# A memory-recurrent attention layer with a gMLP: a split first weight transfer with a warmed TensorE, second waits moved to earlier matmuls, and the context evacuated in eight pieces

## The chip, the cores and the metric

The kernel runs on one core of one Trainium2 chip. The metric is the device time of one execution in microseconds (us). Most executions of one kernel agree within 0.3 per cent, which here is 2.6 us, so single microseconds need several executions.

## The reference, cut to what matters

```python
h  = x + A(layernorm(x))            # x: 1 x 2048 x 512, bf16
h2 = h + B(layernorm(h))

# A: 64 segments of 32 rows, one after the other
for s in range(64):
    hs = concat([mem, xs[s]])                    # 8 memory rows + 32 rows
    q, k, v = hs @ Wq, hs @ Wk, hs @ Wv          # 32 heads of 128
    p = softmax(mask(q @ k.T * 128**-0.5))
    o = (p @ v) @ Wo                             # 40 x 512
    mem = o[:8]                                  # the next segment needs it
    outs.append(o[8:])

# B: gelu(x @ w_in), layernorm of one half, a 2048 x 2048 product along the rows,
#    a gate, and w_out
```

A is a chain: segment s+1 cannot start before the eight memory rows of segment s are there. Everything that does not depend on the memory (the products of the x rows with Wq, Wk and Wv) is done ahead, in the opening for the first 32 segments and as fill between the dependent products later.

## The kernel before: the parts that the change and the argument touch

The kernel writes its own dependencies. Each operation is recorded with the tokens it reads and writes; the waits are worked out at the end. An instruction carries one wait itself; for each further one a separate semaphore instruction is emitted ahead of it.

```python
def emit(self, eng_name, eng, sems, dma_sems):
    for op in self.by_eng[eng_name]:
        for d in op.waits:
            ...                                  # eng.wait_ge(semaphore, value), one per wait
        ins = op.fn(eng)
```

The opening: two x tiles, then the weights in pieces of 1 MB, all issued on the SP queue; two layernorms, whose inverse root runs on POOL; transposes, and one copy per tile.

```python
load_xe(0, 0)
load_xe(1, 1)
for hq in range(4):
    load_w(0, hq)                                # Wq, 1 MB each
...
for j in range(2):
    ln_stats(j)
for j in range(2):
    ln_apply(j)
    xT(j, 6 + j)                                 # four 128 x 128 transposes
    xe_copy(j, 6 + j)                            # one ACT copy
for i in range(8):                               # Q products of both chunks of 16 segments
    for ck in range(2):
        start_group(qkx_mm, qkx_evac, ck, i)
for n in range(8):                               # V products of the first chunk
    ...
    start_v(0, n)
```

The V products (`vx_mm`) are evacuated by ACT and DVE in turn into one of eight rows of a buffer, `part`, and stored to memory from there (`vext_d`).

The end of a step: the probabilities times V (`PV_half`, with 16 matmuls on V and 4 on Vx, the V rows of x, for each half b of the heads), the evacuation of the context into `cT`, the output projection (`Wo`).

```python
PV_half(s, 0)
PV_half(s, 1)
for f in xs[2:4]: f()                            # fill: products of x rows of a later chunk
fill(nw2)
cT_evac(0, "act", (0,))
cT_evac(2, "dve", (0,))
cT_evac(0, "act", (1,))
cT_evac(2, "dve", (1,))
cT_evac(1, "act")                                # both halves, 320 columns
cT_evac(3, "dve")
...
Wo(WOQ, OB, 0, OC)                               # columns 0 to 255, eight quads in the order WOQ
part_evac(s, OB, 0, OC)
Wo(WOQ[:6], OB2, OC, D)
```

## Time and profile before

| | before |
|---|---|
| time, median of 4 executions beside the changed kernel | 868.14 us (867.4 to 869.19) |
| span of the profiled execution | 866.1 us |
| first product of the opening | 7.82 us |
| first V product | 24.51 us |
| first matmul of step 0 | 55.12 us |
| last Vx quad of step 0 to that of step 63 | 623.5 us, the usual step 9.82 us |
| last Vx quad to the last matmul (the MLP) | 176.0 us |
| last matmul to the end | 4.1 us |

The lines that carry these readings stand in the prediction below. How to read it: TensorE's own order of instructions makes 96 per cent of the chain of work that ends last, so what counts is when each quad of matmuls (four column tiles, run together) starts, and not how long an engine is busy. I number the steps from 0 and count a step from the start of its last Vx quad to that of the next step's.

### The profile page before, as it was taken

Reading aid. Unit: us, or ns where it says so; the run is one execution under the profiler, and the core shown is the slowest. Engines: PE = TensorE matmul, PEld = TensorE weight load, DVE = VectorE, ACT = ScalarE, POOL = GpSimd, SP = SyncE. Lnnn points to the kernel's source line nnn. Section 1 sums busy time; section 2 is a strip of 40 time slices with the busy share of each in tenths; the row PEclk is TensorE's granted clock in tenths of the full one; section 3 lists DMA queues with packets and bytes.
Section 4 is the critical chain, followed back from the end, with each engine's and each line's share of the span. In section 5 each row is a group of like instructions: output and inputs, shape, how many; then the busy total and the mean of one; then the engine's idle time right before and its main releaser. Section 6 shows DMA issues by size and latency. Waiting matters only on the chain.

```text
span 866.1 us, 45456 instructions
## 1 busy us (share of the span) xinstructions
PE 849.6 (98%) x22453; PEld 433.9 (50%) x18876; DVE 501.8 (58%) x1246; ACT 467.4 (54%) x1291; POOL 158.6 (18%) x427
## 2 busy tenths in 40 slices
PE   6999999999999999999999999999999999999998
PEld 6664445454445544455445554454554444444443
DVE  3446666666666666666666666566655564363343
ACT  3445666666666666666666666666666655400000
POOL 1621212121212212121211221121211122100000
PEclk9999999999999999999999999999999999999999
DMA  9972232213141211222241313342211690032101
GB/s 323 380 218 72 69 74 74 64 42 85 26 92 29 78 38 50 77 70 57 68 85 31 92 41 93 62 92 58 59 51 42 193 274 16 1 104 77 64 13 39
DMA packets 114180, 75.20 MB, mean 87 GB/s; under 512 B 70712, under 2 KB 99520, under 8 KB 113984
## 3 DMA queue, kind: packets, MB, share of 16 engines
q1 hardware_dynamic: 113840, 72.19, 30.4%
q8 instruction: 164, 2.69, 1.3%
q14 instruction: 32, 0.26, 0.1%
q10 hardware_dynamic: 144, 0.07, 0.0%
HBM read 39.46 MB, written 20.58 MB: 69 GB/s over the span
## 4 chain that ended last, share of the span: by engine, by line
PE 96%; DVE 2%; DMA 1%; issue 1%; SPq 0%; ACT 0%
PE f_ps L280 30%; PE f_ps L660 14%; PE f_ps L281 13%; PE f_ps L1092 11%; PE f_ps L426 3%; PE f_ps L710 3%; PE f_ps L461 3%; PE f_ps L1166 3%; PE f_ps L1054 3%; PE f_ps L574 3%; PE f_ps L1085 3%; PE f_ps L625 3%; PE f_ps L631 1%; PE f_ps L554 1%; PE f_ps L681 1%; DMA f_arena<-in_A_Wq_dram 1%
## 5 line engine op out<-in xcount | busy, mean ns | idle before, releaser
L280 PE MATMUL f_ps<-f_arena,f_hT 128*32 128x512 bf16 (+1 forms) x5120 | 352.8, 337 | 1.7 <-issue 0.5
L281 PE MATMUL f_ps<-f_arena,f_hT 128*32 128x256 bf16 (+1 forms) x3072 | 214.5, 308 | 0.0
L280 PEld LDWEIGHTS f_ps<-f_arena,f_hT 128*32 128x32 bf16 x5120 | 121.0, 96 | 168.8 <-issue 85.6
L518 ACT ACTIVATE f_Tst<-f_ps 128x512 bf16<-128x512 f32 (+1 forms) x320 | 149.9, 510 | 57.6 <-PE f_ps L280 53.9
L660 PE MATMUL f_ps<-f_arena,f_cT 128*32 128x256 bf16 x4096 | 134.6, 273 | 1.4 <-ACT f_cT L645 1.1
L597 POOL TENSOR_TENSOR f_E_sb<-f_R_sb,f_E_sb 128x64 bf16<-128x64 f32 x128 | 48.2, 377 | 378.5 <-ACT f_R_sb L589 378.5
L526 DVE STREAM_TRANSPOSE f_QT<-f_Tst 128x256 uint32<-128x256 uint32 x128 | 57.1, 446 | 94.9 <-ACT f_Tst L518 94.9
L660 PEld LDWEIGHTS f_ps<-f_arena,f_cT 128*32 128x32 bf16 x4096 | 92.7, 95 | 35.6 <-ACT f_cT L645 21.2
L1092 PE MATMUL f_ps<-f_arena 128*128 128x512 bf16 x448 | 100.6, 379 | 0.0
L617 DVE TENSOR_SCALAR f_V_sb<-f_ps 128x512 bf16<-128x512 f32 (+1 forms) x128 | 70.6, 551 | 41.1 <-PE f_ps L280 41.1
L672 ACT ACTIVATE f_part<-f_ps 128x256 bf16<-128x256 f32 x128 | 49.2, 384 | 68.2 <-PE f_ps L660 68.2
L647 DVE TENSOR_SCALAR f_cT<-f_ps 128x160 bf16<-128x160 f32 (+1 forms) x192 | 61.0, 373 | 38.0 <-PE f_ps L631 38.0
L645 ACT ACTIVATE f_cT<-f_ps 128x160 bf16<-128x160 f32 (+1 forms) x192 | 53.0, 348 | 38.9 <-PE f_ps L631 38.9
L1092 PEld LDWEIGHTS f_ps<-f_arena 128*128 128x128 bf16 x448 | 43.8, 98 | 52.7
L526 DVE STREAM_TRANSPOSE f_KT<-f_Tst 128x128 uint32<-128x128 uint32 (+1 forms) x192 | 66.0, 356 | 2.7
L585 ACT ACTIVATE f_R_sb<-f_ps 128x160 f32<-128x160 f32 x128 | 38.9, 304 | 33.5 <-PE f_ps L281 25.6
L1098 DVE TENSOR_TENSOR f_arena<-f_ps,f_arena 128x512 f32<-128x512 f32 x28 | 19.3, 689 | 54.4 <-PE f_ps L1092 52.4
L567 ACT ACTIVATE f_E_sb<-f_ps 128x224 bf16<-128x224 f32 x128 | 45.7, 357 | 0.1
L593 DVE TENSOR_TENSOR f_E_sb<-f_R_sb,f_E_sb 128x160 bf16<-128x160 f32 x128 | 44.7, 350 | 0.0
L589 ACT ACTIVATE f_R_sb<-f_R_sb 128x160 f32<-128x160 f32 x128 | 42.6, 333 | 2.0
L710 PE MATMUL f_ps<-f_arena,f_cTx 128*32 128x512 bf16 x512 | 40.6, 380 | 0.0
L280 PE MATMUL f_ps<-f_arena,f_hTe 128*32 128x512 bf16 x512 | 39.0, 382 | 0.0
(105 smaller groups left out, 1026.7 us busy)
## 6 DMA issues: line engine op xcount, KB each, us to landing
wT_d<-f_wst SPq DMA_DIRECT2D x32, 256.0 KB, 2.7
f_arena<-wT_d SPq DMA_DIRECT2D x32, 256.0 KB, 4.6
f_arena<-in_A_Wq_dram SPq DMA_DIRECT2D x4, 1024.0 KB
f_arena<-in_A_Wv_dram SPq DMA_DIRECT2D x4, 1024.0 KB
f_arena<-in_A_Wk_dram SPq DMA_DIRECT2D x4, 1024.0 KB, 16.0
f_arena<-in_A_Wo_dram SPq DMA_DIRECT2D x4, 1024.0 KB
f_Vx<-vext_d SPq DMA_DIRECT2D x128, 32.0 KB
f_xn<-in_A_x_dram SPq DMA_DIRECT2D x16, 128.0 KB, 2.7
```

Source lines behind the costliest of these rows:

```text
L280: return e.matmul(out, lhsT=lhsT, rhs=rhs, start=start, stop=stop, skip_group_check=True, tile_position=pos)
L281: return e.add_instruction(mybir.InstMatmult(name=nc.get_next_instruction_name(), engine=mybir.EngineType.PE, ins=[e.lower_ap(rhs), e.lowe ...
L518: act(lambda e: e.activation(out=st_.rearrange("p (hp i r) -> p hp i r", i=32, r=2), in_=ps[:, bank, 0:64 * np_].rearrange("p (hp r i) -> ...
L526: dve(lambda e: e.transpose(out=dst, in_=src), reads=tok, writes=[(nm, b, k) for k in halves(b, p0, np_)])
L597: pool(lambda e: e.tensor_tensor(out=ev, in0=rv, in1=ev, op=ALU.mult), reads=[("R", b), ("Ex", b)], writes=[("Ex", b)])
L617: dve(lambda e: e.tensor_scalar(out=dst, in0=src, scalar1=VSC, scalar2=None, op0=ALU.mult), reads=[PB(bank)], writes=tok)
L645: act(lambda e: e.activation(out=dst, in_=src, func=ACT.Copy, scale=UNSC), reads=[PB(PVB[c])], writes=tok)
L647: dve(lambda e: e.tensor_scalar(out=dst, in0=src, scalar1=UNSC, scalar2=None, op0=ALU.mult), reads=[PB(PVB[c])], writes=tok)
L660: pe(lambda e, h=h, g=g, i=i, b=b, c=c: e.matmul(ps[32 * g:32 * g + 32, bank, 0:d1 - d0], lhsT=cTh[:, i, 8:40], rhs=w_o[:, h, d0:d1], star ...
L672: act(lambda e: e.activation(out=part[:, s % 8, d0:d1], in_=ps[:, bank, 0:d1 - d0], func=ACT.Copy), reads=[PB(bank)], writes=[("part", s % ...
L710: pe(lambda e, h=h, g=g, i=8 * qr + bg: e.matmul(ps[32 * g:32 * g + 32, WXB, :], lhsT=cTx[:, rb % 2, i, :], rhs=w_o[:, h, :], start=(i < 4 ...
L1092: pe(lambda e: e.matmul(ps[:, bank, 0:TB], lhsT=z2[:, sc, fb * 128:(fb + 1) * 128], rhs=wTb[tb % 2][:, :, sc, :], start=(sc == 0), stop=(s ...
```

## The change

Its intent is to shorten three things: the opening's start, the wait of the output projection for the context, and the semaphore instructions on TensorE. The core of the diff:

```diff
+        pe = self.by_eng["pe"]
+        for op in pe:
+            while len(op.waits) > 1:
+                d = op.waits[-1]
+                t = next((p for p in reversed(pe[max(0, op.pos - 60):op.pos]) if not p.waits and p.gidx > d.gidx), None)
+                if t is None:
+                    break
+                op.waits.pop()
+                t.waits = [d]
...
+        if mi == 0 and hq == 0:                 # the first Wq piece in two halves of 0.5 MB
+            cm = c0 + 4 * DH
+            sp(lambda e, c0=c0: e.dma_start(ws[:, :, c0:cm], wr[:, :, c0:cm]), writes=["W0"])
...
+    load_xe(1, 1, "act")
     load_xe(0, 0)
-    load_xe(1, 1)
...
+    for _ in range(44):                         # warming matmuls on ones
+        pe(lambda e: e.matmul(ps[:, 1, 0:128], lhsT=onesrc[:, 0:128], rhs=onesrc[:, 0:128], ...
+    ln_bn(0)
+    ln_root(0)                                  # inverse root on ACT: Ln, then Exp of -0.5 of it
...
+    xe_halves(0, 0, (6, 7))                     # half copies on ACT and DVE
...
+        if ck == 1 and n < 4:                   # half of the second chunk's V brought forward,
+            t, tok = (hbuf, xo)[n // 2]...      # into other buffers
...
-    WOQ = ((0, 0), (2, 0), (0, 1), (2, 1), (1, 0), (1, 1), (3, 0), (3, 1))
+    WOQ = ((0, 0), (2, 0), (0, 1), (2, 1), (1, 0), (3, 0), (1, 1), (3, 1))
...
-        cT_evac(1, "act")
-        cT_evac(3, "dve")
+        cT_evac(1, "act", (0,))
+        cT_evac(3, "dve", (0,))
+        cT_evac(1, "act", (1,))
+        cT_evac(3, "dve", (1,))
```

Below, the first block is called the carried waits, the last two (`WOQ` and the evacuations) the pieces, and all between them the opening.

More of the change, by code (lines that the diff above doesn't have):

```diff
@@ L305, in xbuf, with load_xe @@
         return (xn[:, j, :], [("xn", j)]) if j < 2 else (part[:, j, :], [("part", j, 0), ("part", j, 1)])
-    def load_xe(ck, j):
+    def load_xe(ck, j, q="sp"):
         t, tok = xbuf(j)
-        sp(lambda e: e.dma_start(t, xe[CK * ck:CK * ck + CK, XM:SEG, :]), writes=tok)
+        em.add(q, lambda e: e.dma_start(t, xe[CK * ck:CK * ck + CK, XM:SEG, :]), writes=tok, dma=True)
     def load_w(mi, hq):
@@ L314, in load_w @@
         c0, c1 = hq * 8 * DH, (hq + 1) * 8 * DH
+        if mi == 0 and hq == 0:
+            cm = c0 + 4 * DH
+            sp(lambda e, c0=c0: e.dma_start(ws[:, :, c0:cm], wr[:, :, c0:cm]), writes=["W0"])
+            em.mark_const("W0")
+            c0 = cm
         sp(lambda e: e.dma_start(ws[:, :, c0:c1], wr[:, :, c0:c1]), writes=[("W", mi, hq)])
         em.mark_const(("W", mi, hq))
+    load_xe(1, 1, "act")
     load_xe(0, 0)
-    load_xe(1, 1)
     for hq in range(4):
@@ L358, in late_consts, with ln_bn @@
         pool(lambda e: e.tensor_copy(out=mask[:, 224:448], in_=mask[:, 0:224]), reads=["mask"], writes=["mask"])
-    def ln_stats(j):
+    def ln_bn(j):
         t, tok = xbuf(j)
@@ L364, in ln_stats, with ln_root @@
         dve(lambda e: e.bn_stats(out=st1[:, k, :], in_=t), reads=tok, writes=[("st1", k)])
+    def ln_root(j):
+        k = j % 3
+        dve(lambda e: e.bn_aggr(out=mv1[:, k, :], in_=st1[:, k, :]), reads=[("st1", k)], writes=[("mv1", k)])
+        act(lambda e: e.activation(out=rs1[:, k:k + 1], in_=mv1[:, k, 1:2], func=ACT.Ln, bias=EPS), reads=[("mv1", k)], writes=[("rs1", k)])
+        act(lambda e: e.activation(out=rs1[:, k:k + 1], in_=rs1[:, k:k + 1], func=ACT.Exp, scale=-0.5), reads=[("rs1", k)], writes=[("rs1", k)])
+    def ln_stats(j):
+        k = j % 3
+        ln_bn(j)
         dve(lambda e: e.bn_aggr(out=mv1[:, k, :], in_=st1[:, k, :]), reads=[("st1", k)], writes=[("mv1", k)])
@@ L379, in ln_inplace, with xT @@
         ln_apply(j)
-    def xT(j, bank):
+    def xT(j, bank, dcs=range(DC)):
         t, tok = xbuf(j)
-        for dc in range(DC):
+        for dc in dcs:
             pe(lambda e, dc=dc: e.transpose(out=psb[:, bank, dc * 128:(dc + 1) * 128], in_=t[:, dc * 128:(dc + 1) * 128],
@@ L393, in x_flip @@
         sp(lambda e: e.dma_start(xs_d[i], t), reads=rd, writes=[("xs", i)])
-        sp(lambda e: e.dma_start_transpose(out=dst, in_=xs_d[i]), reads=[("xs", i)], writes=[tok])
+        sp(lambda e: e.dma_start_transpose(out=dst, in_=xs_d[i]), reads=[("xs", i)], writes=tok)
     def ring_fill(rb):
@@ L408, in xe_copy, with xe_halves @@
         src = psb[:, bank, 0:512].rearrange("p (dc c) -> p dc c", dc=DC)
-        act(lambda e: e.activation(out=hTe[:, ck % 3, :, :], in_=src, func=ACT.Copy), reads=[PB(bank)], writes=[("hTe", ck % 3)])
+        act(lambda e: e.activation(out=hTe[:, ck % 3, :, :], in_=src, func=ACT.Copy), reads=[PB(bank)],
+            writes=[("hTe", ck % 3, 0), ("hTe", ck % 3, 1)])
+    def xe_halves(ck, j, banks):
+        for hf in range(2):
+            xT(j, banks[hf], (2 * hf, 2 * hf + 1))
+        for hf in range(2):
+            src = psb[:, banks[hf], 256 * hf:256 * hf + 256].rearrange("p (dc c) -> p dc c", dc=2)
+            dst = hTe[:, ck, 2 * hf:2 * hf + 2, :]
+            if hf == 0:
+                act(lambda e, dst=dst, src=src: e.activation(out=dst, in_=src, func=ACT.Copy), reads=[PB(banks[0])], writes=[("hTe", ck, 0)])
+            else:
+                dve(lambda e, dst=dst, src=src: e.tensor_copy(out=dst, in_=src), reads=[PB(banks[1])], writes=[("hTe", ck, 1)])
     def mem0_transpose(bank):
@@ L417, in mem0_transpose, with qkx_mm @@
         act(lambda e: e.activation(out=hT[:, 0, :, 0:M], in_=src, func=ACT.Copy), reads=[PB(bank)], writes=[("hTm", 0, 0), ("hTm", 0, 1)])
-    def qkx_mm(ck, i, bank):
+    def qkx_mm(ck, i, bank, hhs=range(4)):
         mi, q = i // 8, i % 8
         ws = (w_q, w_k)[mi]
-        for hh in range(4):
+        for hh in hhs:
+            wt = "W0" if i < 2 and hh < 2 else ("W", mi, q // 2)
             h = 8 * (q // 2) + 2 * hh + q % 2
@@ L427, in qkx_mm @@
                                                          rhs=hTe[:, ck % 3, dc, :], start=(dc == 0), stop=(dc == DC - 1)),
-                   reads=[("hTe", ck % 3), ("W", mi, q // 2)], writes=[PB(bank)])
+                   reads=[("hTe", ck % 3, dc // 2), wt], writes=[PB(bank)])
     def qkx_evac(ck, i, bank, eng="act"):
@@ L445, in qkx_rows @@
                                           dc == 0, dc == DC - 1, (0, 32 * c)),
-               reads=[("hTe", ck % 3), ("W", mi, 2 * b), ("W", mi, 2 * b + 1)], writes=[PB(bank)])
+               reads=[("hTe", ck % 3, dc // 2), ("W", mi, 2 * b), ("W", mi, 2 * b + 1)], writes=[PB(bank)])
     def qkx_flip(ck, mi, r, b, bank):
@@ L462, in vx_mm @@
                                                        start=(dc == 0), stop=(dc == DC - 1), tile_position=(0, 32 * c)),
-                   reads=[("hTe", ck % 3), ("W", 2, n // 2)], writes=[PB(bank)])
+                   reads=[("hTe", ck % 3, dc // 2), ("W", 2, n // 2)], writes=[PB(bank)])
     def vx_evac(ck, n, bank, eng="act"):
-        if ck < 2:
+        if ck == 1 and n < 4:
+            t, tok = (hbuf, xo)[n // 2][:, n % 2, :], [(("h", "xo")[n // 2], n % 2)]
+        elif ck < 2:
             t, tok = part[:, n, :], [("part", n, 0), ("part", n, 1)]
@@ L758, in fast_path @@
     act(lambda e: e.preload_act_table_set("natural_log_exp_and_others"))
-    for j in range(2):
-        ln_stats(j)
-    for j in range(2):
-        ln_apply(j)
-        xT(j, 6 + j)
-        xe_copy(j, 6 + j)
+    for _ in range(44):
+        pe(lambda e: e.matmul(ps[:, 1, 0:128], lhsT=onesrc[:, 0:128], rhs=onesrc[:, 0:128], start=True, stop=True), reads=["onesrc"], writes=[PB(1)])
+    ln_bn(0)
+    ln_root(0)
+    ln_bn(1)
+    ln_apply(0)
+    ln_root(1)
+    xe_halves(0, 0, (6, 7))
+    ln_apply(1)
+    for hp in range(2):
+        for i in range(2):
+            qkx_mm(0, i, 2 + i, (2 * hp, 2 * hp + 1))
+        if hp == 0:
+            xe_halves(1, 1, (0, 1))
+    qkx_evac(0, 0, 2, "act")
+    qkx_evac(0, 1, 3, "dve")
+    for i in range(2):
+        qkx_mm(1, i, 4 + i)
+        qkx_evac(1, i, 4 + i, ("act", "dve")[i])
     for mi in (2, 1):
@@ L785, in start_v @@
         start_group(vx_mm, vx_evac, ck, n)
-    for i in range(8):
+    for i in range(2, 8):
         for ck in range(2):
@@ L797, in fast_path @@
         start_v(0, n)
-        if n == 1:
+        if n % 2 == 1:
+            start_v(1, n // 2)
+        if n == 2:
             xT(4, 6)
             ring_copy(0, 6)
-        if n == 2:
+        if n == 3:
             xT(5, 7)
             ring_copy(1, 7)
-        if n == 3:
+        if n == 4:
             xT(6, 6)
@@ L814, in fast_path @@
             start_group(qkx_mm, qkx_evac, ck, i)
-    for n in range(8):
+    for n in range(4, 8):
         start_v(1, n)
-        if n % 4 == 3:
-            load_wo(2 + n // 4)
+        if n % 2 == 1:
+            load_wo(n // 2)
     for i in range(12, 16):
@@ L985, in fast_path @@
         if j4 == 1 and 2 <= rb + 2 < RB:
-            late.append(lambda rb=rb: (ln_apply(0), x_flip(0, rb, xn[:, 1, :].rearrange("p (dc c) -> p dc c", dc=DC), ("xn", 1))))
+            late.append(lambda rb=rb: (ln_apply(0), x_flip(0, rb, xn[:, 1, :].rearrange("p (dc c) -> p dc c", dc=DC), [("xn", 1)])))
         if s == 2:
@@ L989, in fast_path @@
         if s == 3:
-            late.append(lambda: (ln_apply(7), x_flip(7, RB, hTe[:, 0, :, :], ("hTe", 0))))
+            late.append(lambda: (ln_apply(7), x_flip(7, RB, hTe[:, 0, :, :], [("hTe", 0, 0), ("hTe", 0, 1)])))
         if j4 == 1 and rb >= 2:
```

## The prediction

> **What bounds the kernel now.** I read the page's first three parts, then the windows by stage, then the timeline of the opening and of one recurrent step, then the rows of single lines.
>
> ```profile
> PE 849.6 (98%) x22453; PEld 433.9 (50%) x18876; DVE 501.8 (58%) x1246; ACT 467.4 (54%) x1291; POOL 158.6 (18%) x427
> DMA  9972232213141211222241313342211690032101
> PE 96%; DVE 2%; DMA 1%; issue 1%; SPq 0%; ACT 0%
> ...
> 0.00:55.10 55.10, 48.02 (x792) 38.78 (x792) 21.95 (x38) 20.66 (x31) 20.05 (x78) 1.00 0.97 329
> 55.10:691.00 635.90, 631.37 (x20834) 316.20 (x17252) 398.44 (x1062) 412.76 (x1201) 122.79 (x315) 1.00 0.28 69
> 691.00:866.10 175.10, 170.25 (x833) 78.95 (x832) 81.41 (x147) 33.97 (x60) 15.78 (x34) 1.00 0.27 77
> ```
>
> TensorE's instruction order sets the end (96% of the chain). The opening projections take 55 us with DMA full (0.97); then 64 recurrent steps take 636 us; the MLP takes 175 us. "PE busy" hides bubbles, since matmul ends are modelled, so I went by the starts of matmuls: four column tiles run together, and such a quad of 512 columns is followed by the next after 215 ns, one of 256 after 109, one of 40 after 25, one of 64 after 28. Anything more is a bubble. A usual step takes 9.81 us. Its middle:
>
> ```profile
> 319.95 0.45 POOL L597 TENSOR_TENSOR f_E_sb<-f_R_sb,f_E_sb 128x64 bf16<-128x64 f32 x1 [0.51 <-ACT f_R_sb L589]
> 320.30 0.21 PE L631 MATMUL f_ps<-f_E_sb,f_Vx 32*128 32x64 bf16 x4
> 320.33 0.28 PE L625 MATMUL f_ps<-f_E_sb,f_V_sb 32*128 32x40 bf16 x16
> 320.50 0.21 PE L631 MATMUL f_ps<-f_E_sb,f_Vx 32*128 32x64 bf16 x4
> 320.73 0.83 ACT L645 ACTIVATE f_cT<-f_ps 128x160 bf16<-128x160 f32 x3 [0.58 <-PE f_ps L631]
> 320.80 0.95 DVE L647 TENSOR_SCALAR f_cT<-f_ps 128x160 bf16<-128x160 f32 x3 [0.57 <-PE f_ps L631]
> 321.08 1.14 PE L660 MATMUL f_ps<-f_arena,f_cT 128*32 128x256 bf16 x32
> ...
> L158 PEldq EVENT_SEMAPHORE  x167: 51/51/51, 7.7 to 822.3; - x167
> L160 PEldq EVENT_SEMAPHORE  x52: 51/51/51, 28.6 to 694.7; - x52
> L645 ACT ACTIVATE f_cT<-f_ps x192: 297/304/444, 62.8 to 686.6; 128x160 bf16<-128x160 f32 x128, 128x320 bf16<-128x320 f32 x64
> L647 DVE TENSOR_SCALAR f_cT<-f_ps x192: 311/325/482, 62.8 to 686.8; 128x160 bf16<-128x160 f32 x128, 128x320 bf16<-128x320 f32 x64
> ```
>
> See two things. The PV products (L625, L631) end in quads that wait for two semaphores, and TensorE has 219 separate semaphore instructions of 51 ns. And the output projection (L660) starts while ACT and DVE are still evacuating the context: its fifth quad starts 186 ns after the fourth (median of 64 steps), not 109, because it waits for ACT's 320-wide piece.
>
> The opening:
>
> ```profile
> 3.49 0.69 DVE L364 BATCH_NORM_STATS2 f_st<-f_xn 128x6 f32<-128x512 bf16 x1 [3.49 <-DMA f_xn<-in_A_x_dram]
> 4.80 0.57 POOL L368 TENSOR_TENSOR f_rs<-f_rs,f_mhalf 128x1 f32<-128x1 f32 x1
> 7.05 0.61 PE L384 MATMUL f_ps<-f_ident,f_xn 128*128 128x128 bf16 x4 [0.57 <-DVE f_xn L374]
> 7.82 6.38 PE L426 MATMUL f_ps<-f_hTe,f_arena 128*128 128x128 bf16 x70 [0.16 <-DMA f_arena<-in_A_Wq_dram]
> ...
> 26.90 0.40 PE L384 MATMUL f_ps<-f_ident,f_part 128*128 128x128 bf16 x4 [0.48 <-DVE f_part L374]
> ```
>
> The first projection waits for 1 MB of Wq until 7.82. Its matmuls start 107 ns apart until 12.7 us, then 56. At 26.04 the last V quad starts, and TensorE waits for DVE's normalization until 26.90.
>
> **What the skill says.** "TensorE: Matmul & The Clock Gate", Part 1: the array runs at half clock until about 3.4 us of sustained activity, in a free-running window, 107 ns a 128-column matmul cold and 56 warm. The trace agrees: 107, then 56, the change 4.9 us after the dense run began. "Perfetto Trace Analysis", Identifying Dependency Chains: instructions that wait on several engines may get EventSemaphore instructions put before them. Agrees: 219 on TensorE, 51 ns each. "VectorE: DVE Perf Modes", the errata section, gives a PSUM read a fixed part plus one cycle an element (172 + FD for ScalarE, 120 + FD for VectorE). Agrees in kind: ACT 304 ns for 160 columns and 443 for 320, so splitting a piece should repeat some 165 ns; but consecutive 160-wide pieces start 184 to 200 ns apart on ACT and 236 on DVE, so most of the fixed part overlaps the neighbour.
>
> **The change, part by part.**
>
> *Eight pieces.* ACT did 160, 160, 320; now 160 four times; DVE likewise; the projection takes the halves in the order in which they come. In the step at 410 us: the first quad starts at .068; ACT starts its third piece at .091, DVE at .246. Split, ACT's halves end near .39 and .57, DVE's near .56 and .80; 0.055 later TensorE may go. Quads four to eight are due at .51, .62, .73 and .84: the first three are ready, the last comes at .85. So the ninth quad, the first of the second half of the columns, starts some 65 to 75 ns earlier than now, where the fifth starts at .587 instead of .51. ACT and DVE finish 40 and 70 ns later; ACT's next work after a projection flip leaves 234 ns before the part evacuation, which moves 75 nearer: enough. 64 x 0.070 = 4.5 us.
>
> *Carried waits.* A second wait is moved to an earlier matmul that had none, so the 51 ns instruction goes. In a step three matmuls have two waits. The one before the scores is hidden under 256-column quads (109 to the next: no bubble). The two at L631 show as 79 ns instead of 25: 54 each, 108 a step. But the work behind them has its own clock. In usual steps the second half's PV starts 101 ns after DVE's normalization ends, where 57 is what a bound start shows; and the last L631 starts 108 ns after POOL's multiply (L597), where bound steps show 60 and without the instruction some 57. So of 97 to 108 ns only about 51 can come out before POOL bounds. About 34 usual steps give 51; some 4 with POOL early give 97; every fourth step (already bound by DVE and POOL) gives about 8; about 10 whose Vx load is late give nothing. 1.7 + 0.4 + 0.1 = 2.2 us; I take 2.0. The context's evacuation follows L631 directly (0.58 to the projection, with or without fill between), so this passes on.
>
> *Opening.* The x tiles are issued on two queues, Wq's first half MB comes alone and is issued 0.6 us earlier, and the inverse root goes from POOL (0.22 + 0.57 and hops) to two ACT operations of about 0.2 (estimate from ACT's smallest rows, 0.18 to 0.19). x at 3.49, statistics to 4.40, root to 4.95, apply 0.41 to 5.4. The 44 warm matmuls run from about 1.08 for 44 x 0.107 = 4.7, to 5.8, so the transposes go at 5.8 and, after half-width copies on ACT and DVE, the first product at about 6.6 (Wq's half MB near 5.8, an estimate from 7.7 for a whole one). That is 1.2 earlier than 7.82. Cold matmuls cost before (12.7 - 7.8)/2 = 2.4; after, the gate should open between 4.5 and 7.9 by the skill's window, so about 0.2 remains: 2.2. V groups of the second chunk fill the wait at 26.04: 0.65. One transpose group now stands in the stream: -0.25. Sum 3.8 us. All matmul work is the same; the rest of the file is not touched.
>
> Together 3.8 + 4.5 + 2.0 = 10.3 us: **868.4 - 10.3 = 858.1**, say 858.
>
> **Rivals.** (1) The opening is held by the loads. For: DMA is at 0.97 and about 386 GB/s until 44 us; the third Wk piece landed at 37.2, pieces are 2.7 us apart, so Wv's first is in near 20 and TensorE will want it at 21. Also the first Wq wait is now carried to the fourth transpose, so a late Wq holds the second copy too. Against: bringing forward half of the second V delays the want for Wk by 3.5 us. If it wins, the opening gives 1.5 to 2 and the time is 860. (2) POOL doesn't bind, and the carried waits give all 108 ns: 6.9 us, time 853.5. Against: bound steps show its 60 ns clearly. Or a wait met costs the same wherever it stands, and they give nothing: 860. (3) The extra two evacuations push ACT and DVE so that the last half comes late: every 10 ns is 0.6 us, and if nothing is won, 862.5. Against: the starts above. (4) The whole is hidden because the recurrence is bound by another engine: 866 or no change; against, DVE and ACT are at 63 to 65% in the steps and wait for TensorE.
>
> **Range and chances.** Independent doubts: opening +-1.5, pieces +-1, waits +-2, Vx loads +-1: together about 3. 855 to 861.5 holds it 8 times in 10. Two per cent is 17.4 us, to 851: it needs rival 2 and more; 0.03. Slower by 2%: 0.01. Same: 0.96.
>
> **What would show it.** First projection at 6.6 and all 56 ns apart from about 6 to 7 us; the opening ending at 51.3 instead of 55.1; no wait for Wv or Wk. In a step: the fifth L660 quad 109 to 120 ns after the fourth, and the ninth some 75 ns earlier than now, counted from the first; semaphore instructions on TensorE nearly gone; the last Vx product 57 ns after POOL's multiply; a usual step at 9.69 instead of 9.81. I am wrong if the last Vx quad starts less than 57 ns after POOL, if a new bubble stands at the eighth quad, or if the MLP's 175 us move.

## The result, and the profile after

The changed kernel took 860.87 us (median of four, 858.82 to 863.35), against 868.14. The ratio is 0.9917, with a 95 per cent interval of 0.9888 to 0.9945; ratios here are the mean time of a kernel's executions over that of the executions of before in the same rounds, so not quite the ratio of the medians. The predicted 858.0 is 2.9 us too low, and the time lies in the range of 855 to 861.5. Of the 10.3 us promised, about 7.3 came.

The page of the changed kernel, first part, the DMA row and the chain:

```profile
PE 845.2 (98%) x22497; PEld 427.6 (50%) x18920; DVE 506.4 (59%) x1312; ACT 471.7 (55%) x1359; POOL 156.3 (18%) x423
DMA  8983222213041211322241313243231690032101
PE 96%; DMA 2%; DVE 1%; issue 0%; SPq 0%; ACT 0%; DVEq 0%
```

See that TensorE still carries 96 per cent, but that DMA has come up from 1 to 2 per cent of the chain. The windows by stage (columns: stretch, its length, busy time and instruction count of PE, PEld, DVE, ACT and POOL, granted clock, DMA share, GB/s):

```profile
0.00:54.44 54.44, 50.43 (x836) 40.78 (x836) 22.32 (x40) 20.89 (x35) 18.26 (x74) 1.00 0.95 323
54.44:683.34 628.90, 624.67 (x20838) 307.89 (x17256) 402.75 (x1126) 416.94 (x1265) 122.34 (x315) 1.00 0.28 70
683.34:859.10 175.76, 170.15 (x833) 78.88 (x832) 81.34 (x147) 33.87 (x60) 15.75 (x34) 1.00 0.26 77
```

The opening, promised at 51.3, ends at 54.4: it gave 0.7 us of the 3.8. The steps gave 7.0, where 6.5 had been promised. The last stretch is 0.7 us longer, but not in the MLP: its matmuls take 175.9 us as before, and the end after the last matmul takes 4.8 us instead of 4.1. That end is between 4.1 and 5.2 us in all traces, without pattern. One usual step in the changed kernel, its middle, to be laid beside the step in the prediction:

```profile
317.17 0.44 POOL L636 TENSOR_TENSOR f_E_sb<-f_R_sb,f_E_sb 128x64 bf16<-128x64 f32 x1 [0.52 <-ACT f_R_sb L628]
...
317.40 0.27 PE L664 MATMUL f_ps<-f_E_sb,f_V_sb 32*128 32x40 bf16 x16
...
317.51 0.20 PE L670 MATMUL f_ps<-f_E_sb,f_Vx 32*128 32x64 bf16 x4
...
317.54 0.29 PE L664 MATMUL f_ps<-f_E_sb,f_V_sb 32*128 32x40 bf16 x16
...
317.67 0.21 PE L670 MATMUL f_ps<-f_E_sb,f_Vx 32*128 32x64 bf16 x4
...
317.95 0.89 ACT L684 ACTIVATE f_cT<-f_ps 128x160 bf16<-128x160 f32 x4 [0.58 <-PE f_ps L670]
318.02 1.02 DVE L686 TENSOR_SCALAR f_cT<-f_ps 128x160 bf16<-128x160 f32 x4 [0.57 <-PE f_ps L670]
...
318.30 1.19 PE L699 MATMUL f_ps<-f_arena,f_cT 128*32 128x256 bf16 x36
```

In the step before, the two Vx quads (L631 there, L670 here) start 0.20 us apart, here 0.16: 40 ns are gone. POOL's multiply ends at 317.61 and the last Vx quad starts at 317.67, 56 ns later, so it is bound by POOL, as foretold. But now look at what follows. ACT takes the context up at 320.73 − 320.50 = 0.23 us after that quad's start before, and at 317.95 − 317.67 = 0.28 us after it here. The 40 ns did not reach the evacuation. The rows of the evacuation by form:

```profile
L684 ACT ACTIVATE f_cT<-f_ps x256: 297/308/323, 62.1 to 679.1; 128x160 bf16<-128x160 f32 x128
L686 DVE TENSOR_SCALAR f_cT<-f_ps x256: 311/315/326, 62.2 to 679.3; 128x160 bf16<-128x160 f32 x128
```

All 256 pieces on each engine are now 160 columns wide and none lasts over 326 ns. There are no semaphore instructions left on TensorE: the rows of that instruction list other engines only.

The chain of waits of the opening of the changed kernel (start, length, what):

```profile
2.41 6.83 DMA f_arena<-in_A_Wq_dram
9.24 0.05 issue
9.29 13.65 PE f_ps L463 x240
...
40.46 6.79 DMA vext_d<-f_part
47.26 0.03 issue
...
47.36 0.70 DVE f_part L512
48.06 0.05 issue
48.10 6.43 PE f_ps L463 x112
```

Two transfers stand in it: the second half of the first Wq piece, where the chain before had the whole piece (from 2.16, 5.52 us long), and a store to memory, which the chain before did not have. The first product starts at 6.83, a microsecond earlier than before, but TensorE then waits until 9.24 for the second half of the split piece. And at 46.5 it stops for 1.6 us (the 1.36 in the view below counts from a modelled end), because DVE and ACT may not write over rows of `part` whose store has not landed:

```profile
44.21 0.60 ACT L510 ACTIVATE f_part<-f_ps 128x512 bf16<-128x512 f32 x1 [2.15 <-DMA vext_d<-f_part]
...
47.36 0.69 DVE L512 TENSOR_SCALAR f_part<-f_ps 128x512 bf16<-128x512 f32 x1 [4.40 <-DMA vext_d<-f_part]
...
48.10 1.07 PE L463 MATMUL f_ps<-f_hTe,f_arena 128*128 128x128 bf16 x16 [1.36 <-DVE f_part L512]
```

That store was issued at 40.46, right behind 1 MB of Wo, and landed at 47.26.

### The profile page after: what moved, and what is told of

Its sections match the earlier page's. It is cut to its first block, busy times and chain, and to the rows that moved or that the text cites. A ratio compares the mean times of both kernels' runs of the same rounds, so it can differ in the third digit from the quotient of the medians.

```text
span 859.1 us, 45449 instructions
## 1 busy us (share of the span) xinstructions
PE 845.2 (98%) x22497; PEld 427.6 (50%) x18920; DVE 506.4 (59%) x1312; ACT 471.7 (55%) x1359; POOL 156.3 (18%) x423
## 4 chain that ended last, share of the span: by engine, by line
PE 96%; DMA 2%; DVE 1%; issue 0%; SPq 0%; ACT 0%; DVEq 0%
PE f_ps L289 30%; PE f_ps L699 13%; PE f_ps L290 13%; PE f_ps L1148 11%; PE f_ps L749 3%; PE f_ps L498 3%; PE f_ps L463 3%; PE f_ps L664 3%; PE f_ps L1222 3%; PE f_ps L1110 3%; PE f_ps L613 3%; PE f_ps L1141 3%; PE f_ps L593 1%; PE f_ps L670 1%; DMA f_arena<-in_A_Wq_dram 1%; DMA vext_d<-f_part 1%
## 5 line engine op out<-in xcount | busy, mean ns | idle before, releaser
L699 PE MATMUL f_ps<-f_arena,f_cT 128*32 128x256 bf16 x4096 | 130.0, 274 | 1.3 <-ACT f_cT L684 1.1
L699 PEld LDWEIGHTS f_ps<-f_arena,f_cT 128*32 128x32 bf16 x4096 | 90.2, 94 | 35.3 <-ACT f_cT L684 22.9
L686 DVE TENSOR_SCALAR f_cT<-f_ps 128x160 bf16<-128x160 f32 x256 | 65.1, 317 | 36.4 <-PE f_ps L670 36.4
L684 ACT ACTIVATE f_cT<-f_ps 128x160 bf16<-128x160 f32 x256 | 57.1, 309 | 36.9 <-PE f_ps L670 36.9
L1154 DVE TENSOR_TENSOR f_arena<-f_ps,f_arena 128x512 f32<-128x512 f32 x28 | 19.3, 690 | 54.4 <-PE f_ps L1148 52.4
```

The costliest lines, as they stand in the source:

```text
L684: act(lambda e: e.activation(out=dst, in_=src, func=ACT.Copy, scale=UNSC), reads=[PB(PVB[c])], writes=tok)
L686: dve(lambda e: e.tensor_scalar(out=dst, in0=src, scalar1=UNSC, scalar2=None, op0=ALU.mult), reads=[PB(PVB[c])], writes=tok)
L699: pe(lambda e, h=h, g=g, i=i, b=b, c=c: e.matmul(ps[32 * g:32 * g + 32, bank, 0:d1 - d0], lhsT=cTh[:, i, 8:40], rhs=w_o[:, h, d0:d1], star ...
```

## The experiments

Twelve runs followed, on four chips, and all gave correct results. Kernels are compared only within the same rounds. This table has them in one place; "gain" is (1 − ratio) times 868 us, and the last two columns are from the profiled execution of each, in us.

| kernel | ratio (95 per cent interval) | gain | first V product | first matmul of step 0 |
|---|---|---|---|---|
| before | 1 | 0 | 24.51 | 55.12 |
| changed kernel | 0.9917 (0.9888 to 0.9945) | 7.2 | 22.86 | 54.46 |
| changed kernel again | 0.9914 (0.9900 to 0.9928) | 7.5 | 22.05 | 53.84 |
| pieces alone | 0.9973 (0.9960 to 0.9986) | 2.3 | 25.91 | 56.52 |
| pieces alone, again | 0.9969 (0.9956 to 0.9983) | 2.7 | 24.79 | 55.39 |
| carried waits alone | 0.9996 (0.9983 to 1.0009) | 0.3 | 24.66 | 55.26 |
| opening alone | 0.9995 (0.9982 to 1.0008) | 0.4 | 22.38 | 52.95 |
| pieces and carried waits | 0.9928 (0.9916 to 0.9941) | 6.2 | 24.84 | 55.44 |
| pieces and carried waits, again | 0.9938 (0.9917 to 0.9959) | 5.4 | 24.09 | 54.69 |
| changed, whole first Wq piece | 0.9945 (0.9931 to 0.9959) | 4.8 | 25.01 | 55.07 |
| changed, free V buffers | 0.9911 (0.9897 to 0.9925) | 7.7 | 24.02 | 54.08 |
| changed, no warming | 0.9936 (0.9921 to 0.9951) | 5.6 | 23.69 | 54.28 |
| changed, more warming | 0.9928 (0.9914 to 0.9941) | 6.2 | 23.03 | 54.76 |
| changed, four waits removed | 0.9909 (0.9894 to 0.9924) | 7.9 | 22.61 | 52.66 |

### The parts, each alone

The pieces alone: the last two blocks of the diff above, put into the kernel before.

> The kernel before with the eight context pieces alone. The prediction's term is -4.5 us; the two traces put the gain at 64 to 75 ns a step, so I expect -4.1 to -4.8 us against before (864 us), the fifth Wo quad 109 to 120 ns after the fourth where before has 186. Rival (the pieces need the earlier context of the carried waits, or push ACT and DVE late): under 2 us. Opening unchanged, first step's first quad at 55.1.

Measured: 865.84 us against 867.80, a gain of 2.3 us, less than expected. The mechanism is as foretold: the fifth Wo quad starts 109 to 110 ns after the fourth in nearly every step, and the steps are shorter. In this one profiled execution the opening was 1.4 us longer than before, though nothing in it was changed: the first Wq piece landed at 9.08 instead of 7.68.

The carried waits alone: the first diff block.

> The kernel before with the carried waits alone. The prediction's term is -2.0 us. From the trace of the changed kernel I now expect about -1 us: the last Vx quad starts earlier by 25 to 50 ns in usual steps, but the context's evacuation starts only some 27 ns earlier, and not at all in steps that flip Q and K rows. Rivals: -2 (the prediction), -6.9 (all 108 ns come out), 0 (a wait costs the same wherever it stands).

Measured: 867.27 against 867.80, a gain of 0.3 us with an interval that holds zero. The prediction's 2.0 is out, and so is the rival of 6.9; the expected 1 is not (the interval ends at 1.5). In the profiled execution the steps took 621.1 us, 2.3 less than before, but the stretch after them took 0.7 us more (176.7) and the end 1.0 more (5.1).

The opening alone: the changed kernel with the carried waits and the pieces undone.

> The changed kernel without the pieces and without the carried waits, so the opening alone. The prediction's term is -3.8 us. The trace of the changed kernel has the first step at 54.46 instead of 55.13, so I expect -0.7 us, at most -1.5. If it gives -2 or more, the opening also shortens the first steps (their Vx loads), which would explain that the steps gained 7.6 us in the one profile where pieces and waits account for about 5.

Measured: 867.01 against 867.80, a gain of 0.4 us, although the profiled execution reached step 0 at 52.95, 2.2 us earlier than before. That execution, too, lost 0.7 us after the steps (176.7) and 0.5 at the end (4.6), so these losses do not belong to the carried waits.

A single time does not show where in a step it was won. I took the medians of each segment of a step over steps 16 to 63, for each place of a step in its group of four (the fill differs by place); a step at its medians is called undisturbed below. Here a step runs from the last Vx quad of the step before to its own, and "memory rows" is the first matmul that forms them. The four lengths of a group:

| ns, places 0, 1, 2, 3 | last Vx quad to first Wo quad | first Wo quad to memory rows | first to last Vx quad | sum of four steps |
|---|---|---|---|---|
| before | 583, 583, 582, 582 | 1632, 1630, 1629, 1632 | 201, 208, 201, 289 | 39,229 |
| pieces | 583, 582, 582, 582 | 1566, 1566, 1562, 1566 | 201, 202, 201, 300 | 38,986 |
| carried waits | 591, 632, 607, 634 | 1633, 1633, 1634, 1634 | 161, 161, 160, 353 | 39,210 |
| both | 591, 633, 607, 634 | 1567, 1567, 1568, 1567 | 160, 160, 160, 352 | 38,947 |
| changed | 591, 634, 607, 633 | 1565, 1565, 1565, 1566 | 159, 160, 160, 351 | 38,923 |

Sixteen such groups make the 64 steps. The pieces save 16 × 243 ns = 3.9 us, all of it between the first Wo quad and the memory rows, where it was predicted (65 ns a step instead of 70). The carried waits save 16 × 19 ns = 0.3 us alone and 16 × 39 ns = 0.6 us on top of the pieces. The table shows why so little: what they take out between the Vx quads (40 ns) comes back, by 8 to 52 ns, between the last Vx quad and the projection. Before, that stretch was 582 ns whatever the fill; with the waits carried it depends on the fill. In the fourth place nothing was taken out: the first Vx quad moves forward there and the last one hardly does. The columns do not make the whole sum; left out is the stretch from the memory rows to the first Vx quad, in which the carried waits take out 101 ns a group (29,478 before, 29,377 with the waits alone), so that 19 ns remain.

### The changed kernel again, and the steps' two parts together

> The changed kernel again, unaltered, as a control beside the other runs of this call. The parts alone measured -2.3 (pieces), -0.4 (carried waits) and -0.5 us (opening), 3.2 together, while the whole measured -7.3. If the parts simply add and the rest was luck of single executions (the rings' lag in the opening and pauses of TensorE that wait for nothing), this gives -4 to -6 us against before. If the parts need each other, it gives -7 again and the kernel with pieces and carried waits but no new opening gives clearly more than 2.7.

> The kernel before with the pieces and the carried waits, without the new opening. From undisturbed steps: pieces 62 ns a step, carried waits 14 to 20 ns more, together 4.8 us in 64 steps. So -4.8 us against before if the steps set the time; less than 3.5 would say that something gives it back. The opening stays at 55.1 to 56.5.

Measured: the whole gives 7.5 us again, and pieces with carried waits give 6.2. So the first guess, that a lucky set of executions made the whole look large, falls, and so does "about 4.8" for the pair: 2.3 and 0.3 alone, 6.2 together. The pieces alone and the pair were each repeated on a further chip.

> The eight pieces alone once more, on another chip. They measured -2.3 us, while undisturbed steps of that trace are shorter by 61 ns, which is 3.9 us over 64 steps; in that one profile the opening was 1.4 us longer because the first Wq piece landed at 9.08. If the parts add, this gives -3 to -4.5. If it gives -2.3 again, pieces alone are worth less than their steps show, and pieces and carried waits need each other.

> Pieces and carried waits without the new opening, once more on another chip. Alone they measured -2.3 and -2.5 (pieces) and -0.4 (waits), together -6.2. From undisturbed steps, by phase of four, pieces are worth 61 ns a step (3.9 us) and the waits 5 to 10 ns (0.3 to 0.6 us). If the undisturbed steps are the whole truth, this gives about -4.5 and the -6.2 was on the lucky side; if -6 comes again, together they are worth more than their undisturbed steps show, and what remains is in the disturbed steps.

Measured: 2.7 for the pieces, 5.4 for the pair. The interval of this second pair (3.6 to 7.2 us) holds the 4.5 us of its undisturbed steps, that of the first (5.1 to 7.3) does not; both intervals of the pieces alone end below their 3.9. By the means, the pair is worth 5.8, the parts 2.5 and 0.3. In undisturbed steps the parts add (4.2 of 4.5 us), so what is left over, some 1.3 us for the pair and as much the other way for the pieces alone, lies outside the undisturbed steps. One thing that differs from execution to execution can be seen in the trace of the kernel before, in its chain of waits:

```profile
560.61 0.23 PE f_ps L280 x2
560.84 0.53 issue
561.37 0.38 PE f_ps L280 x2
```

TensorE stops for half a microsecond in the middle of independent matmuls and waits for nothing that this view shows. The list of the DMA queues shows more: one queue carries instructions (packets, MB, share of the 16 engines' span).

```profile
q8 instruction: 164, 2.69, 1.3%
```

These are 164 packets of 16 KB, and the trace lists 41,555 instructions of TensorE's (matmuls, weight loads and semaphore instructions), so a packet holds about 256 of them. The fourteen traces have 33 pauses of 0.15 to 0.92 us after the last Vx quad of step 0 that no semaphore explains. All 33 stand 193 to 195 instructions past a multiple of 256, counted from the trace's first, and end 1.16 to 1.61 us after a packet of this queue has landed; at such places in general the median is 2.3 to 2.6 us after it, and the least in each trace 1.04 to 1.33. So TensorE very likely waits there for its own next instructions. No run moved these packets; it is what all fourteen traces fit. The changed kernel's first profile has no such pause.

The excess of the mean step over the median of its place, for steps 13 to 63 and scaled to 64, was 3.3 to 4.2 us in the four traces without carried waits and 1.0 to 4.2 in the ten with them (mean 3.8 and 2.6). Of the mean over all fourteen, 2.9 us, 2.5 is lost at those same places of the instruction stream. That points to less of this loss with the waits carried, but the ranges overlap, the number of packets is nearly the same (164 before, 163 with the waits carried), and the kernel with carried waits alone has a low excess and yet gained nothing. So why the two parts are worth more together stays open.

### The opening: the split of the first piece

```diff
-        if mi == 0 and hq == 0:
-            ...                                 # one piece of 1 MB again
```

> The changed kernel with the first 1 MB of Wq as one transfer again. Theory: the split spreads the 16 rings, its second half lands at 9.24 where the whole piece landed at 7.68, and TensorE waits 1.27 us for it. If so, the whole piece lands near 7.7 to 8.3, the first product starts there instead of at 6.83, no wait follows, and the opening ends within 0.5 us of the changed kernel's 54.46, earlier rather than later (53.9 to 54.5), time 0 to -0.6 us against the changed kernel. Rival: the half piece's early start is worth what the prediction says, and the whole piece costs about 1 us (opening ends at 55.4).

Measured: 4.8 us of gain instead of 7.2. My theory, that the split itself cost its 1.27 us, falls, and the rival holds in its direction: the whole piece landed at 8.30 and the V products started at 25.01, 2.1 us later than with the split. But something else was in that trace:

```profile
5.81 0.34 PE L403 MATMUL f_ps<-f_ident,f_xn 128*128 128x128 bf16 x3
8.35 0.23 PE L403 MATMUL f_ps<-f_ident,f_xn 128*128 128x128 bf16 x1 [2.20 <-DMA f_arena<-in_A_Wq_dram]
8.41 0.28 PE L458 MATMUL f_ps<-f_hTe,f_arena 128*128 128x128 bf16 x2
8.96 1.68 PE L458 MATMUL f_ps<-f_hTe,f_arena 128*128 128x128 bf16 x14 [0.27 <-DVE f_hTe L440]
```

The wait for Wq was carried to the fourth transpose, a work that does not need Wq. It held back the second half of the copy too, so the third product came 0.6 us after the first (8.96 against 8.41). And the 14 matmuls there took 1.68 us, not 0.8: the clock had gone cold again. So this run does not price the split alone; the cold clock may be part of its 2.4 us.

### The opening: other buffers for the last V groups

```diff
+        elif ck == 1:                           # second chunk, groups 4 to 7: rows of a buffer
+            t, tok = cTx[...], [("cTxo", n)]    # that is first used at the end of step 0
         elif ck < 2:
             t, tok = part[:, n, :], ...
```

> The changed kernel, with the last four V groups of the second chunk evacuated into buffers that no earlier store reads. Theory: in the changed kernel TensorE stood 1.58 us at 46.5 us because DVE and ACT could not write over rows whose store, queued behind 1 MB of Wo, had not landed. If so that wait is gone, the first step starts at 52.7 to 53.2 instead of 54.46, and the time falls by 0.7 to 1.5 us against the changed kernel (part of it is given back in the first step, which waits for the last Wo piece). Rival: the wait moves to the K weights or the next store, and nothing changes.

Measured: the wait at 46.5 us is gone (the K products ran from 46.83 without a stop), but step 0 began at 54.08, and the gain over the changed kernel is 0.2 us, within the spread. The time was lost at the front this time. The windows of this kernel, one microsecond each (the last three columns are granted clock, DMA share, GB/s):

```profile
7.00:8.00 1.00, 0.45 (x5) 0.29 (x6) 0.46 (x2) 0.00 (x0) 0.00 (x0) 1.00 1.06 393
8.00:9.00 1.00, 1.00 (x16) 1.00 (x15) 0.15 (x1) 0.00 (x0) 0.00 (x0) 0.77 1.07 409
9.00:10.00 1.00, 1.00 (x12) 1.00 (x11) 0.29 (x1) 0.38 (x1) 0.00 (x0) 0.50 1.02 381
10.00:11.00 1.00, 1.00 (x12) 1.00 (x11) 0.00 (x0) 0.69 (x1) 0.00 (x0) 0.50 1.07 403
11.00:12.00 1.00, 1.00 (x13) 1.00 (x11) 0.72 (x1) 0.06 (x1) 0.00 (x0) 0.52 1.06 393
12.00:13.00 1.00, 1.00 (x21) 1.00 (x20) 0.00 (x0) 0.48 (x1) 0.00 (x0) 1.00 1.05 389
```

The clock falls to 0.50 in the window from 8 to 9 and is back at 12. From the fractions, it fell at 8 + (0.77 − 0.50)/0.50 = 8.54 and rose at 11.96: 3.42 us. Twelve matmuls a microsecond start in it, 21 after it. What had come before:

```profile
5.63 0.34 PE L408 MATMUL f_ps<-f_ident,f_xn 128*128 128x128 bf16 x3
7.27 0.23 PE L408 MATMUL f_ps<-f_ident,f_xn 128*128 128x128 bf16 x1 [1.29 <-DMA f_arena<-in_A_Wq_dram]
7.34 0.27 PE L463 MATMUL f_ps<-f_hTe,f_arena 128*128 128x128 bf16 x2
```

The first Wq half landed at 7.22 here, at 6.40 in the first profile of the changed kernel, and TensorE, warmed by then, had 1.3 us with nothing to do. In the repeat of the changed kernel the same wait was 0.86 us and the clock stayed up. The skill's page "TensorE: Matmul & The Clock Gate", Part 1, says that the array falls back to half clock after at least one idle window of about 3.4 us, and that the windows run free of the kernel. The 3.42 us agree. But no full window was idle here: in the window that ended at 8.54 TensorE was busy for about 1.8 of 3.4 us (0.85 us up to 5.97, 0.34 from 7.27, 0.65 from 7.89; 0.4 of it transposes), and that was not enough. Single executions of the changed kernel with a mean clock of 0.997 or 0.998 (863.35 us of the first four, 860.03 of the second) fit such an episode: 3.4 us at half clock lower the mean over 860 us by 0.002. The second of them was not slow, though (median 860.27). In the executions with the whole Wq piece, whose wait is longer, five of six had 0.996 to 0.998.

### The opening: without warming, and with more of it

```diff
-    for _ in range(44):
-        pe(...)                                 # warming matmuls
```

> The changed kernel without the 44 warming matmuls. Prediction's step: the cold clock cost 2.2 to 2.4 us at the start. Then the first matmuls are 107 ns apart again for some 4 to 5 us. But the changed kernel also waits 1.27 us for the second half of the first Wq piece, which a cold start would hide, so I expect the V products to start 1.0 to 1.5 us later than 22.86, and the wait at 46.5 us to shrink by as much: the first step at 54.5 to 55.5, time 0 to +1 us against the changed kernel. Rival: the whole 2.2 us.

Measured: a gain of 5.6 instead of 7.5, so 1.9 us slower, with intervals that overlap a little. In its trace the matmuls are 107 ns apart from 7 to 11 us and V starts at 23.69, 0.8 us later than in the first trace of the changed kernel (a little less than expected); step 0 starts at 54.28, within 0.5 us of the changed kernel's, because the wait for the `part` store shrank to 0.4 us, as expected. The trace thus puts the warming at 0 to 0.4 us by the end of the opening. The rest of the 1.9 us it does not account for: three of the six executions took 860.8 to 861.0 us, three 863.0 to 864.3, and the profiled one, 864.29, has a pause of 1.9 us in step 0, of the kind described above: it stands 193 past a multiple of 256, and TensorE goes on 1.3 us after the packet has landed.

```diff
     xe_halves(0, 0, (6, 7))
+    for _ in range(12):
+        pe(...)                                 # 12 more warming matmuls, which then carry the wait
     ln_apply(1)
```

> The changed kernel with 12 more warming matmuls between the four transposes and the first product. Theory: in three of six traces of the new opening TensorE waits 1.3 us or more for the first Wq piece after the warming matmuls, and the granted clock then falls to 0.50 for 3.4 us; and the carried Wq wait stands at the fourth transpose, which holds the second half of the copy. With the fill the wait falls on a warming matmul, all products are 56 ns apart from the start, the second half of the copy no longer delays the third product, V starts at 21.8 to 22.9 in every execution, and no execution has a clock of 0.997. Time 0 to -1 us against the changed kernel, because the opening then waits for the store at 46.5 us. Rival: nothing changes, since the wait for Wq's second half decides.

(The "three of six" in that expectation was a miscount. The clock fell in two traces, those of the whole piece and of the free buffers.) Measured: a gain of 6.2 us, not better than the changed kernel. The front behaved as foretold: all products ran at 56 ns, the third product came with the first, and no execution had a clock under 0.999. But the second half of the Wq piece landed at 9.39 and TensorE waited 1.24 us for it, so V started at 23.03, just past the expected range. The rival holds: this wait decides.

### Four waits removed together

```diff
+    # 12 more warming matmuls, and the other V buffers, as above
+    qkx_mm(0, 0, 2, (0, 1)); xe_halves(1, 1, ...); qkx_mm(0, 1, 3, (0, 1))
+    for i in range(2): qkx_mm(1, i, 4 + i, (0, 1))   # the second tile's first heads
+    ...                                              # before the second half of Wq is needed
     load_wo(1)
+    load_wo(2); load_vx(0); load_wo(3); load_vx(1)
-    for j in range(2): load_vx(j)
```

> Fill, free buffers for the last V groups, the second x tile's first half of heads ahead of the second Wq piece, and the last two Wo pieces requested before the Vx loads. Theory: what the prediction promised for the opening (3.8 us) was lost to four waits: the first Wq piece and its clock, its second half (1.3 us), the part store (1.6 us) and the last Wo piece in the first step (0.4 us). With all four gone the first step starts at 51.5 to 52.5 and the first two steps are 9.75 us each: -2 to -3 us against the changed kernel, 857 to 858. Rival: the loads hold the opening anyway (a K or V piece, or the Vx load that now comes later), and it stays within 1 us.

Measured: step 0 starts at 52.66, 1.2 to 1.8 us earlier than in the two traces of the changed kernel, just outside the expected range. The time, 860.40 us (a gain of 7.9), is not clearly better than the changed kernel's 7.2 and 7.5. The trace of its front:

```profile
6.81 0.61 PE L463 MATMUL f_ps<-f_hTe,f_arena 128*128 128x128 bf16 x8
7.26 0.39 PE L408 MATMUL f_ps<-f_ident,f_xn 128*128 128x128 bf16 x4
7.48 3.41 PE L463 MATMUL f_ps<-f_hTe,f_arena 128*128 128x128 bf16 x55
11.67 11.01 PE L463 MATMUL f_ps<-f_hTe,f_arena 128*128 128x128 bf16 x193 [0.78 <-DMA f_arena<-in_A_Wq_dram]
```

The wait for the second half is gone and a new one stands at the next Wq piece, which landed at 11.62. After it TensorE runs without a further wait to step 0, so from 11.67 on its own work sets the opening, and not the loads. The rest of the expectation failed as well: step 0 was still 0.35 us longer than the usual step, although the last Wo piece landed at 58.57 instead of 62.79. So it is not the last Wo piece that lengthens step 0, or not it alone.

### Why the landing times vary

Each transfer signals 16 times, once for each DMA engine's share, and a consumer waits for all 16. The first and the last signal of the early Wq transfers:

| kernel | transfer | first of 16 | last of 16 |
|---|---|---|---|
| before | first Wq piece, 1 MB | 7.29 | 7.68 |
| pieces alone (same opening) | first Wq piece, 1 MB | 7.38 | 9.08 |
| changed | second half of it, 0.5 MB | 6.68 | 9.24 |
| changed again | second half of it | 6.70 | 8.29 |
| more warming | second half of it | 7.01 | 9.39 |
| before | last Wk piece | 38.06 | 39.81 |
| changed | last Wk piece | 38.45 | 41.30 |

The first share of a transfer arrives at nearly the same time in all. The last lags by 0.4 to 2.6 us in the early transfers, differently in each execution, and the lag of the changed kernel at 9 us is still there at 41. In the kernel before it grew, from 0.4 to 1.75 us. The kernel before has the same scatter as the changed one (7.63 to 9.08 for the same transfer in the six traces with the old opening), so part of the opening's length, over 1 us, is drawn anew in each execution.

## Why the prediction was right or wrong

The time lies in the range, and the largest term was right in mechanism and nearly in size, but the two others were too large. That the range was met is in part luck: the terms as measured below make 6.0 us, which is 862.1 from 868.14 and outside it; the rest came from a gain that nobody foretold.

- **Pieces, 4.5 us predicted.** Right: 3.9 us in undisturbed steps, 65 ns a step where 70 was foretold, and in the predicted place. The fifth quad starts 109 ns after the fourth instead of 186. No bubble at the eighth quad, though some 20 ns come back at quads seven to nine (116, 111 and 120 ns after the one before, instead of 109). Rival 3 (the last half comes late) falls. The time of the pieces alone shows only 2.3 and 2.7 us of it.
- **Carried waits, 2.0 us predicted.** Mis-sized: 0.3 alone and 0.6 us with the pieces, in undisturbed steps. The step that failed is "the context's evacuation follows L631 directly, so this passes on". The start of the last Vx quad did move, from 326 to 274 ns after the first PV quad, to 56 ns behind POOL as foretold (57), but the evacuation did not move with it: counted from the first PV quad, ACT starts it at 551, 556, 550 and 726 ns before (places 0 to 3) and at 550, 525, 550 and 724 in the changed kernel. The signal that releases it came at 525 to 528 ns before; in the changed kernel it comes at 502 ns in steps whose V block carries four signals of TensorE, and at 528 ns in those that carry a fifth, at the first Vx quad. The skill's page "TensorE: Matmul & The Clock Gate", Part 3, "The cost: per-tile semaphore tail", says that the increments of matmuls serialize, at about 26 ns each. The 26 ns between 502 and 528 look like one of these, but the trace does not bear it out: the fifth signal is there at 360 ns, long before, the four others stand 34 ns apart, and before the change the fifth made a difference of only 3 ns. Why the signal does not follow the quad stays open; no run took a signal away. By time, the waits are worth 0.3 us alone but 3.3 on top of the pieces (5.8 less 2.5, over three chips), which their undisturbed steps do not show.
- **Opening, 3.8 us predicted.** Mis-sized: alone it gains 0.4 us of time; on top of the other two about 1.5 (7.3 of the whole less 5.8 of the pair). Its own terms: the first product did come earlier (6.83 for 7.82, predicted 6.6), the cold matmuls went (56 to 57 ns from the first product on), and the wait at the V transposes went. What failed is the assumption that nothing stands behind them. This was my rival 1, "the opening is held by the loads", with 860 as its time and the remark that the carried Wq wait holds the second copy. It named the pieces of Wk and Wv; it was the second half of the first piece (1.3 us), the `part` store (1.6 us) and in some executions the clock.
- **"No wait for Wv or Wk", "a usual step at 9.69".** The first held, if narrowly: from the prediction's own figures Wv's first piece is due at 37.2 − 6 × 2.7 = 21.0, not 20; it landed at 21.90, and the V products came only at 22.86. The second is 9.73 (38,923 / 4).
- **Rivals 2 and 4.** (By its own sum rival 2 stands at 853.2, not 853.5.) The waits gave neither all nor nothing at their own place, but nearly nothing at the next; no other engine bounds the steps.

The three terms as measured in undisturbed steps and by difference, 3.9 + 0.6 + 1.5 = 6.0, leave 1.3 of the 7.3 us unassigned: the pair of the pieces and waits gains more time than its undisturbed steps do, and the cause of that is not shown.

## What to carry to other kernels

Taking a wait off an instruction helps only as far as its completion signal moves; read the time from the block's start to the release of its consumer, not to its last start. In a stretch where the loads run at full rate, a wait removed can uncover the next transfer, and one transfer counts as landed only when its slowest share has; compare several executions before crediting a microsecond there. A warm clock must be kept warm up to the first real product, and a wait that is moved to an earlier instruction also holds back everything that this instruction feeds. Where an engine stops and no semaphore tells why, count its instructions: it may be waiting for the next block of them.

## What the Trainium skill lacked or had wrong

- "TensorE: Matmul & The Clock Gate", Part 1: the page has the gate close after an idle window. Here it closed after a window of 3.4 us in which TensorE was busy for about 1.8 us, and stayed at 0.50 for 3.42 us. How busy a window must be is not said; the page's other case of closing, by short idles between groups of matmuls, gives no figure for it either.
- The same page and section: the cold start does not show in the profile's clock column. In the kernel before, matmuls are 107 ns apart from 8 to 12 us with a granted clock of 1.00, while the closing at 8.54 us in the kernel with free buffers shows as 0.50.
- "DMA: Bandwidth & Descriptors": it says, in "Two DMAs through the same engine are not ordered", that nothing orders transfers across the 16 engines, and the trace agrees. It does not say how far they drift: the last of the 16 shares of one early load landed 0.4 to 2.6 us after the first, and in the changed kernel the lag lasted over the whole 41 us of loads.
- "Runtime: NRT & Kernel Launch", "Instruction fetch mechanics": it says that instructions are refilled in blocks of 256 and that crossing into the next block is mostly hidden. The blocks agree with the traces, but TensorE paused there for 0.15 to 0.92 us 33 times in fourteen traces, and once for 1.9, and some 2.5 us per 64 steps went there in the mean. What a late block costs is not said.
- "Perfetto Trace Analysis", "Identifying Dependency Chains": it says that the semaphore instructions are put in, and the trace agrees (219, 51 ns each). It does not say that taking them away may gain nothing: 40 ns a step between the two Vx quads gave 5 to 10 ns a step.
